# A fused attention and MLP block on one core: x tiles with their own homes, loads placed between transpositions, and W2 loads tied to W1 items

## The chip, the core and the metric

The kernel runs on one core of a Trainium2 chip. Five engines work on their own instruction queues: TensorE (PE, matrix products; its weight loads are listed as PEld), VectorE (DVE), ScalarE (ACT), GpSimd (POOL) and SyncE (SP), which issues all the kernel's DMAs. The metric is the device time of one execution in microseconds; the profile counts its span from the first to the last instruction of the program.

## The reference

Input x is 2048 rows of 1024. The reference normalizes the rows, runs an attention block and an MLP on the normalized rows, and joins both:

```python
x = A_x
xn = _layernorm(x, axis=-1)
s = _A_ref(xn, A_wqkv, A_wo)                       # 32 heads of 32, softmax(q k^T / sqrt(32)) v, then @ wo
g = _silu(_B_ref(xn, B_w1, B_b1, B_w2, B_b2))      # gelu(layernorm(xn) @ w1 + b1) @ w2 + b2, hidden width 3584
return x + s * g
```

Everything is bf16 in memory; the products accumulate in f32.

## The kernel before

**Tiling.** The 2048 rows are 16 tiles of 128 (`t`), or 8 pairs of 256 (`n`, `qb`, `kp`). The 32 heads are 8 groups of four (`hg`). `xnT` holds the normalized x transposed, 8 blocks of 128 columns (`dc`). The score work is cut into *units* (`unit`): for one head group, one block of 256 queries and one of 256 keys, eight matmuls (line 846) fill four of six PSUM banks, and two ScalarE activations of 1024 columns (line 855) write the exponentials into a `P` buffer. There are 8 x 8 x 8 = 512 units, so about a thousand such activations. Values and row sums are matmuls of `P` (line 612); in head group 0 the first three query blocks sum with eight extra matmuls for each unit (`plain`), later ones mostly by adds on VectorE (`tree`).

**The prologue.** For each tile: load x (`load_x`) into a home `xst`, mean and variance, `rs` = (variance + eps)^-0.5 by a GpSimd power (line 794), normalize on VectorE into one of four `xnb` (`normalize`). Statistics come from two `bn_stats` and a `bn_aggr` on VectorE; for tile `AT` = 1 ScalarE makes them, with a Copy and a Square that also sum (line 769), and VectorE finishes them with three small instructions. Tiles 0 to 3 (`NTR` = 4) are transposed by TensorE (`tr_item`) and copied to `xnT` by ScalarE (line 737); tiles 4 to 15 are transposed by DMA from SyncE (line 752). The homes of x are ten blocks of `hT`, so tiles 10 to 15 take the home of a tile ten before; their loads wait for the normalization of an earlier tile (`first[...]`).

`q_item` and `k_item` make Q and K of head group 0 for one pair in 16 matmuls of 256 columns; the K goes to SBUF by ScalarE (line 722), the Q by VectorE (line 712). `v_item` makes V for head groups 0 and 1 with `wv`. The units of group 0 follow in a written order (`order0`), (0,0), (0,1), (1,0), (1,1), (0,2) and so on, as query block and key block; a key block must be there before its first unit.

**The MLP.** `make_y` loads x rows again into `yst`, normalizes them and transposes them by DMA into `yT`; `w1_item` multiplies by W1 from a ring of three 512 KB buffers and writes `hT`; `w2_item` multiplies by W2 from a ring of four 448 KB buffers. These items are woven into the attention. Buffers are shared over time: the W1 and W2 rings, a part of `hT` and others first hold exponentials of head group 0, which `after(...)` orders.

**What sets the order.** `_Plan` records every operation with its engine, a cost, a priority and its dependencies, then runs a greedy list scheduler (`run`) over them: ScalarE prefers exponentials, TensorE prefers score units that are ready and fills with dense items by position and due time. SyncE's DMAs are ordered by the same planner, with a modelled bandwidth. What comes out is a fixed order of instructions on each engine; `settle` and `emit` add the semaphore waits. So an edit in the prologue can reorder everything behind it. While TensorE would be idle early on, the planner puts filler matmuls (line 668). A part of the program draws on a fixed number to break ties (`seeds`); it is the same in both kernels.

## Time and profile before

| | |
|---|---|
| median of three runs | 1037.83 us (1036.45 to 1039.3) |
| the profiled execution | 1036.92 us, span 1035.1 us |
| TensorE busy | 1006.4 us, 97% |
| ScalarE busy | 1016.2 us, 98% |
| VectorE busy | 941.4 us, 91% |
| GpSimd busy | 11.5 us, 1% |
| first exponential starts | 12.70 us |
| DMA, whole span | 168.01 MB, 162 GB/s on the mean |
| granted TensorE clock | 0.998 |

A timeline line gives the start and the length in us, the engine (PE, PEld, DVE, ACT, POOL; SPq is SyncE issuing DMAs), the source line, the operation, the tile written and those read, the shapes, how many like it follow one another, and in brackets the idle time before the first of them with what ended it. A line of the page's groups gives in the end busy time, mean length, and idle time before. A landing is the time from the issue of a DMA to its completion. A wait on several semaphores is put down to the one that came last.

### The profile page before, as it was taken

What the parts mean: (1) busy time and instruction counts of PE and PEld (TensorE: products, weight loads), DVE (VectorE), ACT (ScalarE), POOL (GpSimd) and SP (SyncE); (2) the same over time, 40 slices, a digit from 0 to 9 for tenths busy, and PEclk for the clock granted to TensorE, in tenths of its full rate; (3) what the DMA queues carried; (4) which work ended last, traced back from release to release, by engine and by line L of the source; (5) the groups of instructions that cost most, each with busy time, mean ns of one, the idle gap of its engine ahead of it and who ended that gap; (6) DMA issues with size and microseconds to landing.
All of it is one profiled execution on the core that took longest, in us unless ns stands there. A gap on an engine that the chain in (4) does not pass through costs nothing.

```text
span 1035.1 us, 31895 instructions
## 1 busy us (share of the span) xinstructions
PE 1006.4 (97%) x14329; PEld 637.8 (62%) x14329; DVE 941.4 (91%) x1321; ACT 1016.2 (98%) x1093; POOL 11.5 (1%) x21
## 2 busy tenths in 40 slices
...
GB/s 204 173 225 109 183 169 165 182 111 154 184 185 166 179 151 220 134 151 193 136 130 175 146 222 168 161 178 153 122 148 160 216 169 87 269 232 121 107 94 60
DMA packets 318200, 168.01 MB, mean 162 GB/s; under 512 B 56688, under 2 KB 306032, under 8 KB 318064
## 3 DMA queue, kind: packets, MB, share of 16 engines
...
q8 instruction: 112, 1.84, 0.8%
...
## 4 chain that ended last, share of the span: by engine, by line
ACT 88%; PE 8%; DVE 2%; DMA 1%; issue 1%; SPq 0%; POOL 0%; DVEq 0%
ACT P L855 81%; PE ps L617 4%; ACT ut L1039 4%; PE ps L612 2%; ACT gw L1066 1%; PE ps L846 1%; ACT P L1156 1%; DVE stats L785 1%; DMA xnT<-gw 0%; DMA hT<-in_A_x_dram 0%; DVE gw L748 0%; DVE PA L872 0%; DVE hT L1369 0%; DVE gw L1067 0%; DVE ut L1036 0%
## 5 line engine op out<-in xcount | busy, mean ns | idle before, releaser
L855 ACT ACTIVATE P<-ps 128x1024 bf16<-128x1024 f32 x988 | 923.0, 1223 | 4.7 <-PE ps L846 4.6
L872 DVE TENSOR_TENSOR PA<-P 128x2048 bf16<-128x2048 bf16 x173 | 210.1, 1217 | 32.0 <-ACT P L855 31.5
L617 PE MATMUL ps<-yT,w1r 128*128 128x256 bf16 x1792 | 228.4, 274 | 0.3
L617 PE MATMUL ps<-w2r,hT 128*128 128x256 bf16 x1792 | 223.6, 274 | 1.4 <-DMA w2r<-in_B_w_dram 1.1
L886 DVE TENSOR_TENSOR PR<-PR,PA 128x2048 bf16<-128x2048 bf16 x173 | 209.4, 1212 | 1.2
L846 PE MATMUL ps<-QKT 32*128 32x256 bf16 x4032 | 200.3, 273 | 9.8 <-ACT P L855 7.8
L617 PEld LDWEIGHTS ps<-yT,w1r 128*128 128x128 bf16 x1792 | 164.4, 98 | 53.3 <-issue 29.7
L617 PEld LDWEIGHTS ps<-w2r,hT 128*128 128x128 bf16 x1792 | 163.1, 98 | 51.4 <-issue 31.2
L846 PEld LDWEIGHTS ps<-QKT 32*128 32x128 bf16 x4032 | 59.9, 92 | 139.2 <-ACT P L855 129.2
L612 PE MATMUL ps<-P,V 128*32 128x256 bf16 (+1 forms) x4080 | 138.0, 272 | 0.0
L617 PE MATMUL ps<-xnT,wqk 128*128 128x512 bf16 (+1 forms) x560 | 131.0, 362 | 3.2 <-DMA xnT<-gw 1.3
L612 PEld LDWEIGHTS ps<-P,V 128*32 128x32 bf16 x4080 | 95.9, 96 | 31.6 <-issue 22.0
L617 PE MATMUL ps<-wv,xnT 128*128 128x256 bf16 (+1 forms) x576 | 87.6, 286 | 0.6 <-DVE hT L1022 0.3
L617 PEld LDWEIGHTS ps<-xnT,wqk 128*128 128x128 bf16 x560 | 49.5, 98 | 53.3 <-issue 14.3
L1022 DVE TENSOR_TENSOR hT<-ps,b1T 128x512 bf16<-128x512 f32 x112 | 76.7, 685 | 2.3 <-PE ps L617 1.5
L872 DVE TENSOR_TENSOR PR<-P 128x2048 bf16<-128x2048 bf16 x60 | 72.9, 1215 | 0.3 <-ACT P L855 0.2
L617 PEld LDWEIGHTS ps<-wv,xnT 128*128 128x128 bf16 x576 | 52.5, 98 | 24.8 <-issue 11.4
L1039 ACT ACTIVATE ut<-ut 128x2048 bf16<-128x2048 bf16 (+1 forms) x33 | 61.8, 1871 | 0.0
L941 DVE STREAM_TRANSPOSE nt<-ps 128x256 f32<-128x256 f32 x63 | 28.0, 444 | 13.8 <-PE ps L612 13.6
L702 DVE CAST QKT<-ps 128x512 bf16<-128x512 f32 x58 | 39.8, 685 | 0.6 <-PE ps L617 0.2
L1041 DVE TENSOR_TENSOR hT<-ut,hT 128x2048 bf16<-128x2048 bf16 (+1 forms) x33 | 34.7, 1052 | 0.2
L1036 DVE TENSOR_TENSOR ut<-hT 128x2048 bf16<-128x2048 bf16 (+1 forms) x33 | 34.8, 1053 | 0.1
...
## 6 DMA issues: line engine op xcount, KB each, us to landing
w1r<-in_B_w_dram SPq DMA_DIRECT2D x112, 512.0 KB, 4.5
w2r<-in_B_w_dram SPq DMA_DIRECT2D x128, 448.0 KB, 4.6
...
```

Of the source, the lines that this page charges most:

```text
L612: ins = e.matmul(dst(j), lhsT=lhsT(j), rhs=rhs(j), start=start, stop=stop, tile_position=(0, 32 * j), skip_group_check=True)
L617: return e.matmul(dst, lhsT=lhsT, rhs=rhs, start=start, stop=stop, skip_group_check=True)
L702: dve(lambda e: e.tensor_copy(QKT[sl][:, which, tq * 512:(tq + 1) * 512], bank(it.bank)), c_ps(512), [], [(nm, sl, 2 * tq), (nm, sl, 2 * t ...
L846: ins = e.matmul(bank(b0[j], kk * 256, (kk + 1) * 256), lhsT=QKT[sl][32 * j:32 * j + 32, 1, kb * 128:(kb + 1) * 128], rhs=QKT[sl][32 * j:3 ...
L855: x = act(lambda e, h=h: e.activation(Pt[pi][:, 2 * h:2 * h + 2].rearrange("p j k q -> p (j k q)"), ps[:, pr[h] * 1024:(pr[h] + 1) * 1024] ...
L872: return dve(lambda e: e.tensor_tensor(dst[:].rearrange("p u j q -> p (u j) q"), src[:].rearrange("p u j k q -> p (u j) k q")[:, :, 0, :], ...
L886: return dve(lambda e: e.tensor_tensor(fl3(pr), fl3(pr), fl3(PA[i]), op=ALU.add), c_b16(2048), [("PA", i), tok], [tok], 3.2)
L941: dve(lambda e: e.transpose(nt_t[:], bank(pv.bank, 256, 512)), c_ps(256) + 120, [], [("nt",)], prio, pv)
L1022: dve(lambda e: e.tensor_tensor(hT[:, hs], bank(it.bank).rearrange("p (k t) -> p k t", k=2), b1T[:, 2 * pi:2 * pi + 2].unsqueeze(2).to_bro ...
L1036: dve(lambda e: e.tensor_tensor(u_, x_, x_, op=ALU.mult), c_b16(n), hs_, [("ut", ui)], gp)
L1039: act(lambda e: e.activation(u_, u_, ACT.Tanh, scale=GC), c_acts(n), [("ut", ui)], [("ut", ui)], ga)
L1041: dve(lambda e: e.tensor_tensor(x_, u_, x_, op=ALU.mult), c_b16(n), [("ut", ui)] + hs_, hs_, gp)
```

## The change

Seven edits:

1. Each x tile has its own home: ten in `hT` as before, four in the two `PR` buffers, two in the `yst` buffers. The first real users of `PR` and `yst` wait for the reads of these tiles.
2. Tiles 4 to 11 are loaded at once (before: 4 to 9). Tiles 12 and 13 are loaded once tile 7 is normalized, 14 and 15 once tile 9 is; the order on SyncE comes out as: tiles 4 to 11, transposes 4 and 5, `wv`, transposes 6 and 7, tile 12, transposes 8 and 9, tiles 13 and 14, transposes 10 and 11, tile 15, transposes 12 to 15. Before it was: tiles 4 to 9, `wv`, transposes 4 and 5, tiles 10 and 11, transposes 6 to 9, tiles 12 to 15, transposes 10 and 11, one `wqk`, the first two `yst`, transposes 12 to 15.
3. The first load of `wv` waits for the normalization of tile 5; the K weights of head group 1 wait for that of tile 15 (before: 9).
4. `AT` = (1, 3): the statistics of tile 3 are made on ScalarE as well.
5. The first pair's Q and K are made tile by tile in one item (`qk_first`), with 128-column matmuls, the K in bank 1; `k_item(1)` also works tile by tile. The planner may put a TensorE transposition into an open dense item.
6. The `yst` loads of chunk 0 no longer wait for tile 11; those of chunk 1 wait for W1 item 4.
7. The four W2 loads of the first W2 item wait for W1 items 4, 6, 8 and 10. On SyncE they come behind w1 loads; before, all four stood behind the third w1 load.

```diff
@@ -317,6 +317,13 @@
                 use = "v"
             elif d_ok:
                 use = "d"
+            tq, th = self.dense["tr"], heads["tr"]
+            if use is None and S["do"] is not None and th < len(tq) and tq[th].chunks[0].left == 0 and tq[th].chunks[0].ready <= t:
+                heads["tr"] += 1
+                tq[th].k = 1
+                S["mode"] = "d"
+                commit(tq[th].chunks[0], t)
+                return
             if use is None:
                 nxt = min(nxt, v_at, d_at)
                 bf = bank_for() if S["do"] is None and S["pvo"] is None and nxt > t + 250 and t > self.fill0 else None
@@ -498,7 +505,7 @@
         o_d = nc.dram_tensor("o_scratch", (HG, 128, S), BF16).ap()
 
         NP, NPX, NPA, NH, NW1R, NW2R = 10, 16, 3, 20, 3, 4
-        NTR, NWARM, NG0, AT = 4, 8, 3, 1
+        NTR, NWARM, NG0, AT = 4, 8, 3, (1, 3)
         ident = sb("ident", [128, 128], BF16)
         ones = sb("ones", [128, 32], BF16)
         xnT = sb("xnT", [128, DC, S], BF16)
@@ -544,6 +551,10 @@
             Pt.append(h_flat[:, (3 + i) * 2048:(4 + i) * 2048].rearrange("p (j k q) -> p j k q", j=4, k=2))
         NXS = 10
         xst = [h_flat[:, i * 1024:(i + 1) * 1024] for i in range(NXS)]
+        for i in range(2):
+            pr_flat = PR[i][:].rearrange("p u j q -> p (u j q)")
+            xst += [pr_flat[:, 0:1024], pr_flat[:, 1024:2048]]
+        xst += [yst_t[i][:] for i in range(2)]
         xnb = [gw[:, i * 1024:(i + 1) * 1024] for i in range(4)]
         iota_i = ut_t[0][:].rearrange("p a b -> p (a b)")[:, 0:256].bitcast(I32)
 
@@ -617,13 +628,13 @@
             return e.matmul(dst, lhsT=lhsT, rhs=rhs, start=start, stop=stop, skip_group_check=True)
 
 
-        XS = lambda t: ("xst", t % NXS)
+        XS = lambda t: ("xst", t)
 
         def fl3(t):
             return t[:].rearrange("p u j q -> p (u j q)")
 
         def load_x(t, extra=()):
-            dma(f"x{t}", lambda e: e.dma_start(xst[t % NXS], x2[t * 128:(t + 1) * 128, :]), 262144, [], [XS(t)],
+            dma(f"x{t}", lambda e: e.dma_start(xst[t], x2[t * 128:(t + 1) * 128, :]), 262144, [], [XS(t)],
                 rate=390.0, prio=2, occ=500, lat=2450, extra=extra)
 
         nqk = {"n": 0}
@@ -635,17 +646,16 @@
             dma(f"wqk{i}", lambda e: e.dma_start(wqk[i][:], src), 262144, [], [("wqk", i)], prio=2, rate=228.0, extra=extra)
             return i
 
-        def load_v(pr):
+        def load_v(pr, extra=()):
             src = A_wqkv[:, 2 * D + pr * 256: 2 * D + (pr + 1) * 256].rearrange("(c p) n -> p c n", p=128)
-            dma("wv", lambda e: e.dma_start(wv[:], src), 524288, [], [("wv",)], prio=2, rate=200.0)
+            dma("wv", lambda e: e.dma_start(wv[:], src), 524288, [], [("wv",)], prio=2, rate=200.0, extra=extra)
 
         for t in range(NTR):
             load_x(t)
         wk0 = load_qk(0, 1)
         wq0 = load_qk(0, 0)
-        for t in range(4, NXS):
+        for t in range(NTR, 12):
             load_x(t)
-        load_v(0)
         pool(lambda e: e.iota(iota_i, pattern=[[1, 128]], base=0, channel_multiplier=-1), 300, [], [("ut", 0)])
         dve(lambda e: e.tensor_single_scalar(ident[:], iota_i, 0, op=ALU.is_equal), 220, [("ut", 0)], [("ident",)], 0)
         dve(lambda e: e.memset(ones[:], 1.0), 90, [], [("ones",)], 0)
@@ -715,12 +725,27 @@
 
         def k_item(n):
             it = _Item("pro", 0.01 * n)
-            for dc in range(DC):
-                def fn(e, b, dc=dc):
-                    return mm(e, bank(b, 0, 256), wqk[wk0][:, dc, :], xnT[:, dc, n * 256:(n + 1) * 256], dc == 0, dc == DC - 1)
-                chunk(it, fn, Q256, [("xnT", 2 * n, dc), ("xnT", 2 * n + 1, dc), ("wqk", wk0)])
+            for lo, w in ((0, 128), (128, 128)) if n < 2 else ((0, 256),):
+                for dc in range(DC):
+                    def fn(e, b, dc=dc, lo=lo, w=w):
+                        at = n * 256 + lo
+                        return mm(e, bank(b, lo, lo + w), wqk[wk0][:, dc, :], xnT[:, dc, at:at + w], dc == 0 and lo == 0, dc == DC - 1)
+                    chunk(it, fn, Q256 if w == 256 else Q128, [("xnT", 2 * n + i, dc) for i in range(lo // 128, (lo + w) // 128)] + [("wqk", wk0)])
             act(lambda e: e.activation(QKT[0][:, 1, n * 256:(n + 1) * 256], bank(it.bank, 0, 256), ACT.Copy), c_act(256), [],
                 [("K", 0, n)], -1, it)
+            return it
+
+        def qk_first():
+            it = _Item("pro", -0.001)
+            for lo, d0, d1 in ((0, 0, 8), (128, 0, 4), (128, 4, 8)):
+                for k, wi in ((0, wq0), (1, wk0)):
+                    for dc in range(d0, d1):
+                        def fn(e, b, dc=dc, lo=lo, k=k, wi=wi):
+                            return mm(e, bank(k or b, lo, lo + 128), wqk[wi][:, dc, :], xnT[:, dc, lo:lo + 128],
+                                      dc == 0 and lo == 0, dc == DC - 1)
+                        chunk(it, fn, Q128, [("xnT", lo // 128, dc), ("wqk", wi)], [("S", 0, 1)] if k else ())
+            dve(lambda e: e.tensor_copy(QKT[0][:, 0, 0:256], bank(it.bank, 0, 256)), c_ps(256), [], [("Q", 0, 0)], 0, it)
+            act(lambda e: e.activation(QKT[0][:, 1, 0:256], bank(1, 0, 256), ACT.Copy), c_act(256), [("S", 0, 1)], [("K", 0, 0)], -1)
             return it
 
         def tr_item(t):
...
-            first[t] = dve(lambda e: e.tensor_scalar(xnb[t % 4], xst[t % NXS], mv[:, t, 0:1], lnp[:, t, 1:2],
+            first[t] = dve(lambda e: e.tensor_scalar(xnb[t % 4], xst[t], mv[:, t, 0:1], lnp[:, t, 1:2],
...
@@ -762,33 +787,35 @@
                 plan.readers.setdefault(x, []).extend(got)
 
         for n in range(NPR):
+            if n >= 6:
+                for t in (2 * n, 2 * n + 1):
+                    load_x(t, [first[7] if n == 6 else first[9]])
             groups = [(2 * n,), (2 * n + 1,)] if n < 2 else [(2 * n, 2 * n + 1)]
             for ts in groups:
-                if ts == (AT,):
+                if ts[0] in AT:
+                    a_ = ts[0]
                     for k, f, sc in ((0, ACT.Copy, 1.0 / D), (1, ACT.Square, D ** -0.5)):
-                        act(lambda e, k=k, f=f, sc=sc: e.activation(
-                            fl3(PA[0])[:, k * 1024:(k + 1) * 1024], xst[AT], f, scale=sc, accum_out=mv[:, AT, k:k + 1]),
-                            c_acts(1024) + 93, [XS(AT)], [("st", AT, k)], 1)
-                    dve(lambda e: e.tensor_tensor(lnp[:, AT:AT + 1, 2], mv[:, AT:AT + 1, 0], mv[:, AT:AT + 1, 0], op=ALU.mult), 65,
-                        [("st", AT, 0)], [("s2",)], 0.95)
-                    dve(lambda e: e.scalar_tensor_tensor(lnp[:, AT:AT + 1, 0], mv[:, AT:AT + 1, 1], EPS, lnp[:, AT:AT + 1, 2], op0=ALU.add,
-                                                         op1=ALU.subtract), 65,
-                        [("st", AT, 1), ("s2",)], [("ve", AT)], 0.95)
-                    dve(lambda e: e.tensor_tensor(mv[:, AT:AT + 1, 1], mv[:, AT:AT + 1, 1], lnp[:, AT:AT + 1, 2], op=ALU.subtract), 65,
-                        [("st", AT, 1), ("s2",)], [("mv", AT)], 1.1)
+                        act(lambda e, k=k, f=f, sc=sc, a_=a_: e.activation(
+                            fl3(PA[a_ // 2])[:, k * 1024:(k + 1) * 1024], xst[a_], f, scale=sc, accum_out=mv[:, a_, k:k + 1]),
+                            c_acts(1024) + 93, [XS(a_)], [("st", a_, k)], 1)
+                    dve(lambda e, a_=a_: e.tensor_tensor(lnp[:, a_:a_ + 1, 2], mv[:, a_:a_ + 1, 0], mv[:, a_:a_ + 1, 0], op=ALU.mult), 65,
+                        [("st", a_, 0)], [("s2", a_)], 0.95)
+                    dve(lambda e, a_=a_: e.scalar_tensor_tensor(lnp[:, a_:a_ + 1, 0], mv[:, a_:a_ + 1, 1], EPS, lnp[:, a_:a_ + 1, 2],
+                                                                op0=ALU.add, op1=ALU.subtract), 65,
+                        [("st", a_, 1), ("s2", a_)], [("ve", a_)], 0.95)
+                    dve(lambda e, a_=a_: e.tensor_tensor(mv[:, a_:a_ + 1, 1], mv[:, a_:a_ + 1, 1], lnp[:, a_:a_ + 1, 2], op=ALU.subtract),
+                        65, [("st", a_, 1), ("s2", a_)], [("mv", a_)], 1.1)
                 for t in ts:
-                    if t == AT:
+                    if t in AT:
                         continue
-                    if t >= NXS:
-                        load_x(t, [first[2 * n - 5]])
                     for c in range(2):
-                        dve(lambda e, t=t, c=c: e.bn_stats(stats[:, t, c, :], xst[t % NXS][:, c * 512:(c + 1) * 512]),
+                        dve(lambda e, t=t, c=c: e.bn_stats(stats[:, t, c, :], xst[t][:, c * 512:(c + 1) * 512]),
...
-                if ts != (AT,):
+                if ts[0] not in AT:
...
@@ -797,9 +824,12 @@
                     normalize(t, rs)
             if n < NTR // 2:
                 plan.dense["tr"] += [tr_item(2 * n), tr_item(2 * n + 1)]
-            if n < NG0:
-                pro_q.append(q_item(n))
-            pro_q.append(k_item(n))
+            if n == 0:
+                pro_q.append(qk_first())
+            else:
+                if n < NG0:
+                    pro_q.append(q_item(n))
+                pro_q.append(k_item(n))
...
+        load_v(0, [first[5]])
...
-             rss + [("mv", t) for t in range(NT)], [("s2",)], 2)
+             rss + [("mv", t) for t in range(NT)], [("s2",), ("s2", AT[0]), ("s2", AT[1])], 2)
...
@@ -963,7 +994,7 @@
 
 
         def proj(hg, w):
-            wk = load_qk(hg, 1, [first[9]] if hg == 1 else ())
+            wk = load_qk(hg, 1, [first[NT - 1]] if hg == 1 else ())
...
@@ -984,17 +1015,18 @@
...
+        w1_ev = {}
...
-        def load_w2(q, r):
+        def load_w2(q, r, extra=()):
...
-            dma(f"w2{i}", lambda e: e.dma_start(w2r[:, i], src), 458752, [], [("w2", i)], lat=3100.0)
+            dma(f"w2{i}", lambda e: e.dma_start(w2r[:, i], src), 458752, [], [("w2", i)], lat=3100.0, extra=extra)
...
@@ -1002,7 +1034,7 @@
             for t2 in range(2):
...
                 dma(f"yx{t2}", lambda e, t=t, t2=t2: e.dma_start(yst_t[t2][:], x2[t * 128:(t + 1) * 128, :]), 262144, [],
-                    [("yst", t2)], rate=390.0, extra=[first[11]] if c == 0 else ())
+                    [("yst", t2)], rate=390.0, extra=[w1_ev[4]] if c == 1 else ())
...
@@ -1019,7 +1051,7 @@
...
-            dve(lambda e: e.tensor_tensor(hT[:, hs], bank(it.bank).rearrange("p (k t) -> p k t", k=2),
+            w1_ev[p] = dve(lambda e: e.tensor_tensor(hT[:, hs], bank(it.bank).rearrange("p (k t) -> p k t", k=2),
...
@@ -1112,12 +1144,15 @@
                     it = w1_item(s_[1], s_[2])
                 else:
                     for r in range(4):
-                        w2slot[(s_[1], s_[2], r)] = load_w2(s_[2], r)
+                        w2slot[(s_[1], s_[2], r)] = load_w2(s_[2], r, [w1_ev[(4, 6, 8, 10)[r]]] if s_[1] + s_[2] == 0 else ())
                     it = w2_item(s_[1], s_[2])
                 it.pos = pos
                 (mq if s_[0] == "w1" else plan.dense["w2"]).append(it)
 
 
+        for i in range(2):
+            after([("PR", i)], [XS(10 + 2 * i), XS(11 + 2 * i)])
+            after([("yst", i)], [XS(14 + i)])
         pvs = [_Item("pv") for _ in range(NG0)]
         order0 = [(0, 0), (0, 1), (1, 0), (1, 1), (0, 2), (1, 2), (2, 0), (2, 1)]
         for kp in range(3, NKP):
```

## The prediction

> **What bounds the kernel now.** I read the page first, then ScalarE (ACT) in order of time, then who made it wait. The page:
>
> ```profile
> span 1035.1 us, 31895 instructions
> ...
> PE 1006.4 (97%) x14329; PEld 637.8 (62%) x14329; DVE 941.4 (91%) x1321; ACT 1016.2 (98%) x1093; POOL 11.5 (1%) x21
> ...
> q8 instruction: 112, 1.84, 0.8%
> ...
> ACT 88%; PE 8%; DVE 2%; DMA 1%; issue 1%; SPq 0%; POOL 0%; DVEq 0%
> ...
> L855 ACT ACTIVATE P<-ps 128x1024 bf16<-128x1024 f32 x988 | 923.0, 1223 | 4.7 <-PE ps L846 4.6
> ```
>
> ScalarE is busy 98%, nearly all of it exponentials, and the chain runs through it. What the change can win is therefore ScalarE's idle time, 18.9 us. The timeline of ScalarE alone (start, length, idle before) shows where it lies:
>
> ```profile
> 4.22 1.06 ACT L769 ACTIVATE PA<-hT 128x1024 bf16<-128x1024 bf16 x1 [2.00 <-DMA hT<-in_A_x_dram]
> ...
> 7.39 1.02 ACT L737 ACTIVATE xnT<-ps 128x1024 bf16<-128x1024 bf16 x1 [0.98 <-PE ps L733]
> 9.01 2.07 ACT L737 ACTIVATE xnT<-ps 128x512 bf16<-128x512 bf16 x3 [0.60 <-PE ps L733]
> 11.81 0.38 ACT L722 ACTIVATE QKT<-ps 128x256 bf16<-128x256 f32 x1 [0.72 <-PE ps L617]
> 12.70 1.02 ACT L855 ACTIVATE P<-ps 128x1024 bf16<-128x1024 f32 x1 [0.51 <-PE ps L846]
> ...
> 16.66 4.69 ACT L855 ACTIVATE P<-ps 128x1024 bf16<-128x1024 f32 x5 [0.51 <-PE ps L846]
> 22.55 0.38 ACT L722 ACTIVATE QKT<-ps 128x256 bf16<-128x256 f32 x1 [1.19 <-PE ps L617]
> ...
> 37.96 1.02 ACT L855 ACTIVATE P<-ps 128x1024 bf16<-128x1024 f32 x1 [0.73 <-PE ps L846]
> ...
> 64.32 3.77 ACT L855 ACTIVATE P<-ps 128x1024 bf16<-128x1024 f32 x4 [1.11 <-PE ps L846]
> 69.80 31.39 ACT L855 ACTIVATE P<-ps 128x1024 bf16<-128x1024 f32 x34 [1.71 <-PE ps L846]
> ```
>
> From 69.8 us to the last 8 us no gap is listed: in hundred-microsecond windows ScalarE is busy 99.98 to 100.00 of 100. The last 45 rows of the built order are the same for TensorE, VectorE and SyncE, and so are ScalarE's last 19; so a microsecond won before 70 us should arrive at the end. Removable are the gaps from 7.39 to 69.80, 8.3 us with the 0.22 at 15.77.
>
> The last two gaps come from TensorE, which stops inside a block of eight matmuls and waits for nothing:
>
> ```profile
> 61.29 0.28 PE L612 MATMUL ps<-V,ones 128*32 128x256 bf16 x2
> ...
> 63.10 0.40 PE L612 MATMUL ps<-V,ones 128*32 128x256 bf16 x6 [1.53 <-issue]
> ...
> 69.03 0.40 PE L612 MATMUL ps<-P,ones 128*32 128x256 bf16 x6 [1.70 <-issue]
> ```
>
> Between these stops lie 128 matmuls and 128 weight loads, 256 instructions. The page's 112 packets of 16 KB on q8 are one for each 256 of TensorE's 28,658. So these are waits for instructions: the packets that end them begin at 60.42 and 66.50 in the trace, 4.1 and 3.4 us after TensorE crossed the boundary before, and TensorE goes on 1.5 us after each packet's end. From 67 us on no such stop recurs; later boundaries lie some 10 us apart and most packets begin within 0.5 us. At 60 to 64 us the DMA moved 333 GB/s, and SyncE had just queued this:
>
> ```profile
> 57.87 2.13 SPq L1004 DMA_DIRECT2D yst<-in_A_x_dram  x2
> 60.04 0.43 SPq L991 DMA_DIRECT2D w1r<-in_B_w_dram  x1
> 60.51 7.85 SPq L997 DMA_DIRECT2D w2r<-in_B_w_dram  x4
> ```
>
> **The change part by part.** The sum is against the profiled execution: 1036.92 us, span 1035.1, 0.91 below the median 1037.83 of the three runs.
>
> *Tile 3's statistics go to ScalarE, the first pair goes tile by tile.* Removed from VectorE: two bn_stats (0.6 each), an aggregate (0.11) and the +eps (0.06), 1.4 us; added, three small ones at 0.07. Added on ScalarE: what tile 1 costs there, 4.22 to 6.40, 2.18 us. I lay it out by the built order: sums for 3 at 6.32 (x3 landed at 6.19), xnT of tile 0 at 7.45 (was 7.39), squares for 3 at 8.37, xnT of tile 1 at 9.42 (9.01), xnT of 2 at 10.5 (10.0), K copy 11.55 (11.81), xnT of 3 at 12.25 (13.62), first exponential 13.2 (12.70), second K copy 14.1 (15.77), second exponential 14.4 (14.52), third 15.3 (16.66). So the new work fills idle time, delays the first exponential 0.5 and brings the third 1.35 us earlier. The 48 matmuls of 128 columns for 24 of 256 (0.06 each by the fillers' spacing, against 0.11) cost TensorE nothing. The Q copy moves behind a bn_stats on VectorE, to 12.05; it lies under the xnT of tile 3.
>
> *Transposes of tiles 4 and 5.* They are issued when normalized, about 0.7 us earlier (14.9 against 15.65), since VectorE is freer. The second took 4.4 us to land with two x loads beside it and 2.8 when four ran alone; now wv's load is issued behind it. It lands at 19.2 to 20.7 (was 21.41). Eight exponentials are done at 20.8, so the third K copy starts between 20.8 and 21.85; I take 21.1. After it I count the 0.5 us before a score unit again. Ninth exponential: 22.0 against 23.75, gain 1.75 (bounds 1.0 and 1.95).
>
> *Loads in steps.* The 0.73 gap at 37.96 follows the transposes of tiles 10 and 11, issued right behind four x loads:
>
> ```profile
> DMA to landing us min/median/max: 6.1/6.4/6.6
> ```
>
> Four others, at 21 to 27 us, took 2.8. They landed 2.4 and 3.3 us after the last x load. In the new order two x loads (13, 14) stand directly before them and the issue is at about 27.4: landing near 33.5 instead of 37.11, when ScalarE, 2 us ahead, needs the K at about 33. I take 0.3 of the 0.73 (bounds 0 and 0.7). Tiles 12 to 15 follow as now, without a gap before and hence none counted.
>
> *wv behind those transposes.* It lands at 17.7 plus 4.7 to 6.2 us, 22.4 to 23.9; the V matmuls ahead of the seventh unit want it by 24.1. Cost nothing; the cover is thin, and each microsecond past it is one on ScalarE, up to 1. The wqk and first y loads also move back, but the y rows land with about 1 us to spare and are normalized only for W1 items that began at 71.86. The homes in PR and yst change only addresses.
>
> *W2 and second y loads after W1 items.* They leave 2.3 MB out of the rush at 58 to 68 us. In the built order both boundaries still lie after the 24th and the 26th unit, now some 2.2 us earlier, and only three w1 loads and wv precede them; the first two w1 loads are issued near 51.5. The packet wanted at 58.9 should come at 57.7 to 59.7, the one wanted at 64.5 long before. Of 2.82 us I take 2.3 (bounds 0, if the packets come as late as now, and 2.82). In their new place each W2 load is 448 KB, 1.5 us at 300 GB/s, in front of w1 loads that landed 1.4 to 4.3 us before use at 100 to 122 us: nothing, or 0.5 where it just misses.
>
> Sum: 1.75 + 0.3 + 2.3 = 4.35 gained. 1036.92 - 4.35 = 1032.6 on the profile's scale, 1033.5 on the median's; I say 1033.2.
>
> *Where the notes speak against it.* TensorE stood 1.53 and 1.70 us at a boundary of 256 instructions. The Trainium skill (Runtime: NRT & Kernel Launch, "Instruction fetch mechanics") says that crossing such a boundary is "mostly hidden", and gives TensorE a buffer of eight blocks. By this nothing would be won from the W2 move, and the sum would be that of the first rival. In the trace a packet begins after its boundary and is for the next one, so I follow the rows. The skill's page DMA: Bandwidth & Descriptors ("Queues, rings and completion order") adds that each engine takes turns between queues; then a fetch would hardly wait behind SyncE's backlog, and the backlog would not be the cause. The 4.1 and 3.4 us against under 0.5 with a light load speak for the backlog, without proving W2's part; the rival below has its price.
>
> **The rivals.**
> - *The fetch waits stay.* Something other than W2 makes the packets late, or wv and w1 do it as well: the packet at 60.42 began when only wv, wqk, y transposes and w1 had been queued at its request. Only the prologue's 2.05 is won: 1034.9, on the median's scale 1035.8. For it: the first stop; against it: the second stop, with only W2, y and one w1 load outstanding.
> - *The prologue gives nothing.* ScalarE's 2.18 us come before the first exponential, and the transposes of 5 and 11 land as late as now. Then 2.3 is won: 1034.6 (1035.5). Against it: the walk above wins 1.35 before any DMA transpose matters.
> - *Slower: W1 starves.* W2 loads took 6.8 us to land at the median before 100 us, one 8.4. If each of the four holds a w1 load behind it for 8.4 - 4.2 us, less about 2 us of slack, TensorE, which runs in order, stops about 2.2 us four times, and the scores queued behind stop ScalarE: 8.8 - 4.35 = 4.4 us slower, 1041.3. It decides from a hold of about 1.1 us over the slack, four times. Against it: DMA share is 0.54 at 60 to 100 us, and no wait for w1 is listed anywhere.
>
> **How the numbers follow.** Forecast 0.68, fetch waits stay 0.12, no prologue gain 0.08, slower 0.12. The range reaches down to all removable idle time less the statistics, 8.3 - 2.2 = 6.1 (1030.8; I write 1030.5), and up to past the two half gains, 1037. The bound of 0.3% is 3.1 us. Nine tenths of the forecast's chance and a quarter of the half gains lie beyond it: faster 0.66. The half gains' rest and the forecast's tail are within: 0.23. Slower 0.11.
>
> **What would show it.** Right: ScalarE's third exponential near 15.3 and ninth near 22; no "issue" idle over 0.6 us on TensorE at 50 to 70 us; no listed gap on ScalarE after 66. Wrong: statistics of tile 3 holding up xnT of tile 1 by more than 0.5; a gap of over 1 us before the third K copy; TensorE waiting for w1 or wv; new gaps past 70 us, where the whole middle is ordered anew.

## The result and the profile after

The changed kernel takes 1039.46 us (median, 1037.2 to 1040.7); the kernel before, on the same chip, took 1036.45. The ratio is 1.002, 95% interval [1.0012, 1.0029]: slower by 0.2%, where I forecast 1033.2 us and a range up to 1037. By the measure of 2% that is no change. But 4.35 us were expected to be won, so some 6 us are to be explained.

The profiled execution took 1040.15 us (before: 1036.92). From its page:

```profile
span 1038.3 us, 31853 instructions
...
PE 998.3 (96%) x14271; PEld 636.7 (61%) x14341; DVE 938.3 (90%) x1320; ACT 1018.1 (98%) x1097; POOL 11.6 (1%) x21
...
ACT 83%; PE 10%; DVE 3%; DMA 2%; issue 1%; POOL 0%; DVEq 0%; another core or an unknown queue 0%; POOLq 0%
...
L886 ACT ACTIVATE P<-ps 128x1024 bf16<-128x1024 f32 x988 | 922.9, 1221 | 4.3 <-PE ps L877 4.2
```

ScalarE is still the bound and its exponentials cost the same (922.9 us). It is busy 1.9 us more, mostly with the statistics of tile 3. TensorE ran 14,341 matmuls (by its weight loads; some matmul records are missing) against 14,329: twelve more, a number that will matter. ScalarE in order of time (start, length, idle before):

```profile
13.14 1.02 ACT L886 ACTIVATE P<-ps 128x1024 bf16<-128x1024 f32 x1
14.04 0.39 ACT L734 ACTIVATE QKT<-ps 128x256 bf16<-128x256 f32 x1
14.31 6.55 ACT L886 ACTIVATE P<-ps 128x1024 bf16<-128x1024 f32 x7
22.30 0.38 ACT L734 ACTIVATE QKT<-ps 128x256 bf16<-128x256 f32 x1 [1.45 <-PE ps L628]
23.41 3.77 ACT L886 ACTIVATE P<-ps 128x1024 bf16<-128x1024 f32 x4 [0.73 <-PE ps L877]
...
36.05 1.02 ACT L886 ACTIVATE hT<-ps 128x1024 bf16<-128x1024 f32 x1 [0.97 <-PE ps L877]
...
48.70 1.02 ACT L886 ACTIVATE w1r<-ps 128x1024 bf16<-128x1024 f32 x1 [0.81 <-PE ps L877]
...
59.90 9.30 ACT L886 ACTIVATE P<-ps 128x1024 bf16<-128x1024 f32 x10 [1.55 <-PE ps L877]
70.09 6.67 ACT L886 ACTIVATE P<-ps 128x1024 bf16<-128x1024 f32 x7 [0.90 <-PE ps L877]
...
1032.97 0.60 ACT L1396 ACTIVATE PR<-ps 128x512 bf16<-128x512 f32 x1 [4.58 <-PE ps L628]
```

The walk to the eighth exponential came out to 0.1 us. Then the third K copy waits 1.45 us, two gaps follow that the kernel before had smaller or not at all, and the two gaps near 60 and 70 us are still there. The last wait has become 4.58; in the kernel before it was

```profile
1029.53 0.60 ACT L1361 ACTIVATE PR<-ps 128x512 bf16<-128x512 f32 x1 [2.76 <-PE ps L617]
```

TensorE in the changed kernel at those places:

```profile
21.22 1.81 PE L628 MATMUL ps<-xnT,wqk 128*128 128x256 bf16 x15 [1.74 <-DMA xnT<-gw]
...
35.40 0.27 PE L628 MATMUL ps<-xnT,wqk 128*128 128x256 bf16 x1 [1.17 <-DMA xnT<-gw]
...
58.79 0.29 PE L623 MATMUL ps<-P,ones 128*32 128x256 bf16 x3 [1.39 <-issue]
...
68.99 0.29 PE L623 MATMUL ps<-P,ones 128*32 128x256 bf16 x3 [1.05 <-issue]
...
1028.80 0.39 PE L623 MATMUL ps<-P,ones 128*32 128x128 bf16 x15
1030.39 0.22 PE L623 MATMUL ps<-P,ones 128*32 128x128 bf16 x1 [1.20 <-issue]
```

These are waits on DMA transpositions (tiles 5 and 11), the two instruction stops, and a third stop ahead of the last matmul of the last group, on the path to the end. Some words for what follows: a *packet* is a transfer of 16 KB, 256 instructions, on TensorE's instruction queue q8; a *boundary* is a place in TensorE's program where one such block of 256 ends; an *instruction stop* is idle time of TensorE at a boundary, listed as "issue".

ScalarE's idle time by stretch (width of the window less ScalarE's busy time in it, in us; the wait near the end apart). The last two columns are experiments told below:

| stretch, us | before | after | after, 48 fillers fewer | before, 36 fillers fewer |
|---|---|---|---|---|
| 0 to 13 | 5.54 | 3.29 | 3.51 | 5.84 |
| 13 to 26 | 1.92 | 2.17 | 1.36 | 1.06 |
| 26 to 46 | 0.73 | 1.05 | 0.57 | 0.18 |
| 46 to 56 | 0 | 0.81 | 0 | 0 |
| 56 to 75 | 2.92 | 2.45 | 0.52 | 0 |
| 75 to 112 | 0 | 1.02 | 0.13 | 0 |
| 112 to 1020 | 0.04 | 0.08 | 0.58 | 0.18 |
| the wait near the end | 2.76 | 4.58 | 2.75 | 2.76 |
| ScalarE busy, in all | 1016.2 | 1018.1 | 1017.5 | 1015.5 |

Before 13 us the change fills 2.25 us of idle time, nearly all with the new work (ScalarE's 1.9 us more). After that it wins only 0.47 (56 to 75) and loses 0.25 + 0.32 + 0.81 + 1.02 + 1.82.

### The profile page after: what moved, and what is told of

It reads as the page before. It is cut to its first block, busy times and chain, and to the rows that moved or that the text cites. A ratio compares the mean times of both kernels' runs of the same rounds, so it can differ in the third digit from the quotient of the medians.

```text
span 1038.3 us, 31853 instructions
## 1 busy us (share of the span) xinstructions
PE 998.3 (96%) x14271; PEld 636.7 (61%) x14341; DVE 938.3 (90%) x1320; ACT 1018.1 (98%) x1097; POOL 11.6 (1%) x21
## 4 chain that ended last, share of the span: by engine, by line
ACT 83%; PE 10%; DVE 3%; DMA 2%; issue 1%; POOL 0%; DVEq 0%; another core or an unknown queue 0%; POOLq 0%
ACT P L886 76%; PE ps L628 6%; ACT ut L1071 4%; PE ps L623 2%; PE ps L877 2%; ACT gw L1098 1%; ACT P L1191 1%; DMA xnT<-gw 1%; DMA yst<-in_A_x_dram 1%; DMA w2r<-in_B_w_dram 1%; PE ps L678 0%; DVE PA L903 0%; DVE hT L1054 0%; DVE PR L917 0%; DVE stats L812 0%
## 5 line engine op out<-in xcount | busy, mean ns | idle before, releaser
L886 ACT ACTIVATE P<-ps 128x1024 bf16<-128x1024 f32 x988 | 922.9, 1221 | 4.3 <-PE ps L877 4.2
L628 PE MATMUL ps<-xnT,wqk 128*128 128x512 bf16 (+2 forms) x530 | 119.1, 351 | 8.0 <-DMA xnT<-gw 2.9
```

Of the source, the lines that this page charges most:

```text
L628: return e.matmul(dst, lhsT=lhsT, rhs=rhs, start=start, stop=stop, skip_group_check=True)
L886: x = act(lambda e, h=h: e.activation(Pt[pi][:, 2 * h:2 * h + 2].rearrange("p j k q -> p (j k q)"), ps[:, pr[h] * 1024:(pr[h] + 1) * 1024] ...
```

## The experiments

All kernels that follow leave only such matmuls out as write nothing that is used (warm-up matmuls and the fillers that keep TensorE running while it would wait); none leaves out work of the reference. Ratios are to the kernel before on the same chip, which took 1036.1 to 1037.2 us there; kernels of different chips are compared by ratio. A time inside a profile is one execution's: the kernel before and the first kernel of experiment 2 run the same instructions up to 57 us, and their exponentials stand 0.2 to 0.4 us apart there; so smaller differences between two profiles are not read. Several kernels also differ in more than the part that is asked about, since an edit that adds, drops or reorders matmuls shifts what the later boundaries fall on.

### 1. The last block of instructions

My theory on the end: the twelve extra matmuls push a boundary between two 256-instruction blocks into the last group. I took seven warm-up matmuls out of the changed kernel, and put twelve into the kernel before.

```
         def warm_fn(e, b):
-            for _ in range(NWARM):
+            for _ in range(1):
...
-            for _ in range(NWARM):
+            for _ in range(20):
```

The first edit is in the changed kernel, the second in the kernel before. `NWARM` itself stays 8, so the planner writes the same order.

> The changed kernel, with 7 of its 8 warm-up matmuls at the start left out (they write nothing that is used); the planned order is otherwise the same on every engine. Theory 'boundary at the end': the changed kernel has 14341 matmuls against 14329, so TensorE's last boundary of 256 instructions falls into the last block of row-sum matmuls, where it stood 1.20 us; with 7 fewer the program ends before it. Then that stop is gone, the last idle time of ScalarE falls from 4.58 to about 2.8 us and the time by 1.5 us, to about 1038.0. Rival 'late work on VectorE or in the out stores': the end stays at 4.58 us and the time does not change (within 0.3 us). In the early part the boundaries lie 7 matmuls further on in the code; both expect stops of 1 to 1.5 us near 58 and 69 us as before.

> The kernel before, with 20 warm-up matmuls instead of 8, so 14341 in all; nothing else changes. Theory 'boundary at the end': a stop of about 1.2 us appears in the last block of row sums, ScalarE's last idle time rises from 2.76 to about 4.5 us, and the time rises by 1.5 us. Rival 'other late work': no change of the end. The two stops at 61 and 67 us stay in both, within 0.5 us, their place 12 matmuls earlier in the code.

Changed kernel with one warm-up: 1037.76 us, 1.001 [1.0001, 1.002]. The last wait:

```profile
1032.94 0.60 ACT L1396 ACTIVATE PR<-ps 128x512 bf16<-128x512 f32 x1 [2.76 <-PE ps L628]
```

So 1.8 us of the 4.58 were the boundary, in the profile; in the medians half of the loss, some 1.0 us. Nothing else of this profile can be used to size the change: it is the slowest of the kernel's executions (1040.42 us), with a granted TensorE clock of 0.5 for 3.4 us from 37.4 us on. The kernel before with twelve more: 1037.6, 1.0009 [1.0, 1.0018]. Its last wait is 3.19, not 4.6: there the boundary lies ahead of the last two matmuls of the kernel, where TensorE waits for VectorE in any case, and it cost 0.4 us; what makes up the rest of the 0.9 is not known. The mechanism holds; its price depends on what the boundary falls on.

### 2. The later W2 and second y loads, alone and undone

```
-                        w2slot[(s_[1], s_[2], r)] = load_w2(s_[2], r)
+                        w2slot[(s_[1], s_[2], r)] = load_w2(s_[2], r, [w1_ev[(4, 6, 8, 10)[r]]] if s_[1] + s_[2] == 0 else ())
...
-                    [("yst", t2)], rate=390.0, extra=[first[11]] if c == 0 else ())
+                    [("yst", t2)], rate=390.0, extra=[first[11]] if c == 0 else [w1_ev[4]] if c == 1 else ())
```

The first kernel puts this into the kernel before. The second takes it out of the changed kernel (with one warm-up).

> The kernel before with the MLP part of the change alone: the four W2 loads of the first W2 item wait for W1 items 4, 6, 8 and 10, the second y loads for W1 item 4. The prologue is that of before. Theory 'W2 and y loads delay the instruction packets': both stops of TensorE at 61 and 67 us shrink below 0.5 us, ScalarE loses its gaps of 1.11 and 1.71 us, and stands 2.3 to 2.8 us earlier at 80 us. Rival 'wv, y transposes and w1 loads delay them': the first stop stays at 1 us or more, the second shrinks to 0 to 1; ScalarE stands 0.5 to 1.7 us earlier at 80 us. The new order after 80 us may give some of it back: the changed kernel lost 1.35 us there at its 91st exponential.

> The changed kernel without its MLP part (W2 and second y loads as early as the planner wants), and 7 warm-up matmuls fewer so that the end has no boundary. Theory 'the MLP part wins': stops at 58 to 70 us grow from 2.4 to 3 us or more against the changed kernel. Rival 'it is neutral': the stops stay at 2 to 2.5 us. Theory 'order of W1 and W2 work costs 1.35 us at the 91st exponential': without the MLP part that loss is gone. The time against the kernel before: 0 to +1.5 us.

Alone: 1036.12, 0.9994 [0.9984, 1.0005]. The instruction stops fell from 3.2 us to 0.8, and ScalarE's idle time at 56 to 75 us from 2.92 to 0.55: the 2.3 us of the prediction, in the profile. The median shows 0.7 us won, with an interval that takes in no change at all.

```profile
56.95 0.40 PE L612 MATMUL ps<-P,ones 128*32 128x256 bf16 x6 [0.37 <-issue]
62.59 0.40 PE L612 MATMUL ps<-V,ones 128*32 128x256 bf16 x6 [0.44 <-issue]
```

Undone in the changed kernel: 1038.54, 1.0018 [1.0006, 1.003], against 1.001 with it; the stops at 50 to 72 us are 3.7 us in sum against 2.0. Both pairs point to a gain and neither median is clear of the noise; nothing here says that this part makes the change slow. ScalarE's idle time at 75 to 112 us, 1.02 in the changed kernel, is nothing without this part.

### 3. Loads, homes, compute: one part at a time

Five kernels ask which other part loses. (a) All x loads and wv issued at once, ahead of the first transposition, instead of in steps (here and in (b) with one warm-up matmul, to be compared with the 1.001 of experiment 1):

```
-        for t in range(NTR, 12):
+        for t in range(NTR, 10):
+            load_x(t)
+        load_v(0)
+        for t in range(10, 16):
             load_x(t)
...
-        load_v(0, [first[5]])
```

> The changed kernel with one part undone in another way: the loads of all x tiles and of wv are issued at once, ahead of the first DMA transposition (order x4 to x9, wv, x10 to x15), instead of in steps between the transpositions; and one warm-up matmul instead of eight, so that no fetch boundary lies in the last block of matmuls (the warm-up matmuls write nothing that is used). Theory A, loads beside a transposition delay its landing: the transpositions of tiles 5, 10 and 11, which took 4.9, 5.6 and 5.2 us from issue to landing, take about 2.8 to 3.3 us; the ScalarE gaps at 22.3 and 23.4 us (1.45 and 0.73) shrink by 1 us or more in sum and the one at 36.05 (0.97) goes; exponentials 10 to 43 come 1 to 2 us earlier than in the changed kernel, and the time is 1 to 2 us below that of the changed kernel with one warm-up matmul (1037.76), so 1036 to 1036.8. Theory B, a transposition has to wait for all transfers that were issued before it: the first pair (tiles 4 and 5) now lands later than 21.2 us, the gap ahead of the third K copy grows by 1 us or more and the time is 1038 to 1040. Theory C, the transpositions are slow by themselves: they take 5 us as before, and nothing moves by more than 0.5 us.

1038.85, 1.0028 [1.0017, 1.0038], the highest ratio of all. Theory B held for the first pair and A for the later ones:

```profile
26.33 0.38 ACT L737 ACTIVATE QKT<-ps 128x256 bf16<-128x256 f32 x1 [5.66 <-PE ps L628]
27.98 3.77 ACT L885 ACTIVATE P<-ps 128x1024 bf16<-128x1024 f32 x4 [1.26 <-PE ps L876]
```

Tile 4's transposition, issued at 14.70, landed at 22.70: the last x load before it was under way until 20.43, an instruction packet followed until 21.66. Tiles 8 and 9, with nothing about, took 2.7 and 2.8. But tiles 10 and 11 took 4.5 and 4.1 us with no load anywhere near; only a packet (35.94 to 37.49) lay between the issue of tile 10's transposition and its landing. That row did not fit my theory, and led to experiment 5.

(b) The changed kernel with tiles 14 and 15 in the third probability buffer instead of the two yst buffers. The first y loads then need not wait for tile 15:

```
-        xst += [yst_t[i][:] for i in range(2)]
+        xst += [PA[2][:].rearrange("p u j q -> p (u j q)")[:, i * 1024:(i + 1) * 1024] for i in range(2)]
...
-                    [("yst", t2)], rate=390.0, extra=[w1_ev[4]] if c == 1 else ())
+                    [("yst", t2)], rate=390.0, extra=[first[11]] if c == 0 else [w1_ev[4]] if c == 1 else ())
```

> The changed kernel with other homes for tiles 14 and 15 (the third probability buffer PA[2] instead of the two yst buffers), and the first two y loads again wait only for the normalised tile 11, as before the change; one warm-up matmul instead of eight. Theory A, the y chain moved into the time of the fetch packets keeps the two instruction stops at 58.8 and 69.0 us (1.39 and 1.05 us): the y loads land near 39 instead of 50 to 51 us, the first two w1 loads are issued before 56 us, and the issue stops of TensorE between 50 and 70 us fall to 1.2 us or less in sum; exponentials 55 to 86 come about 1.2 to 2 us earlier than in the changed kernel, and the time is 1036 to 1036.8 against the 1037.76 of the changed kernel with one warm-up matmul. Rival B, the stops follow where the 16 KB blocks end and wv alone, not y: the stops stay above 2 us in sum and the time stays within 0.5 us of 1037.76.

1035.24, 0.9992 [0.9984, 1.0001], against 1.001: 1.8 us won, more than hoped. TensorE's instructions are the same in the same order as in the changed kernel with one warm-up, so the boundaries fall on the same work. SyncE in the changed kernel, and then with the other homes (start, time to issue):

```profile
46.45 1.05 SPq L1036 DMA_DIRECT2D yst<-in_A_x_dram  x2
...
48.03 3.40 SPq L855 DMA_DIRECT2D b2b<-in_B_b_dram  x1
...
51.95 3.47 SPq L1041 DMA_TRANSPOSE yT<-yst  x1
55.47 0.58 SPq L651 DMA_DIRECT2D wv<-in_A_wqkv_dram  x1
...
58.70 1.71 SPq L1023 DMA_DIRECT2D w1r<-in_B_w_dram  x2
```

```profile
32.47 1.76 SPq L1036 DMA_DIRECT2D yst<-in_A_x_dram  x2
...
49.63 2.97 SPq L1041 DMA_TRANSPOSE yT<-yst  x1
52.65 0.58 SPq L651 DMA_DIRECT2D wv<-in_A_wqkv_dram  x1
...
55.83 1.64 SPq L1023 DMA_DIRECT2D w1r<-in_B_w_dram  x2
```

The y loads go out 14 us earlier, and what queues behind them 2 to 3 us. ScalarE's idle time at 56 to 75 us is 0.40 us.

(c) The kernel before with the compute part alone (statistics of tiles 1 and 3, the first pair tile by tile), and (d) the same with the later W2 loads; both with four warm-ups, homes and loads of x as before.

```
-        NTR, NWARM, NG0, AT = 4, 8, 3, 1
+        NTR, NWARM, NG0, AT = 4, 8, 3, (1, 3)
...
-            pro_q.append(k_item(n))
+            if n == 0:
+                pro_q.append(qk_first())
+            else:
+                if n < NG0:
+                    pro_q.append(q_item(n))
+                pro_q.append(k_item(n))
```

> The kernel before with the compute part of the change alone: ScalarE statistics of tiles 1 and 3, Q and K of the first pair tile by tile, K of the second pair in two halves, and transpositions of the first tiles taken as soon as they are ready. Homes and loads of the x tiles, the y, w1 and W2 loads stay as before. Four warm-up matmuls instead of eight, so that no fetch boundary lies in the last block of matmuls. Theory A, the compute part wins what was predicted of it and the loads in steps lose it again: the ninth exponential starts 1.5 us earlier than before (22.2 against 23.75), exponentials 16 to 49 about 1.0 to 1.7 us earlier too, the instruction stops at 61 and 67 us stay (2.5 to 3 us in sum), and the time is 1034.8 to 1035.8 against the 1036.45 to 1036.8 of before. Rival B, the win is lost at the next late transposition whatever the loads do: by exponential 34 less than 0.5 us is left, and the time is within 0.5 us of before.

> The kernel before with the compute part and the part that makes the W2 and the second y loads later; homes and loads of the x tiles as before, four warm-up matmuls instead of eight. It leaves out of the change only the x tiles' own homes and the loads in steps. Theory A, the two parts win independently: 1.5 us of the compute part and the 0.3 to 2.2 us that the later W2 loads alone gave, so 1033 to 1035, with less than 1 us of instruction stops on TensorE between 50 and 70 us. Rival B, the second win goes when the first comes (the stops reappear, because the fetch packets are wanted earlier and still come at the same time): 1035 to 1036.5, with stops of 2 us or more in sum.

(c): 1035.07, 0.9996 [0.9986, 1.0006]; (d): 1035.41, 0.9995 [0.9986, 1.0004]. In (c) the fourth exponential comes 1.56 us earlier than before, the tenth still 0.90, the 43rd 0.76. At the 49th it is 2.08, but the added 1.3 us are not the compute part's: TensorE's stops are 1.2 us in sum, not the 3.2 of the kernel before that I expected to stay, with the W2 loads in their old place. So in the profile the compute part wins about half of what A has, and the ratio's interval takes in nothing won. In (d) the stops go (0.4 us), but no second win shows.

(e) The late y loads by themselves, put into (d):

```
-                    [("yst", t2)], rate=390.0, extra=[first[11]] if c == 0 else [w1_ev[4]] if c == 1 else ())
+                    [("yst", t2)], rate=390.0, extra=[first[15]] if c == 0 else [w1_ev[4]] if c == 1 else ())
```

> The kernel before with the compute part and the later W2 loads (which took 1035.4 us), and with the first two y loads made to wait for the normalised tile 15 instead of tile 11; homes and loads of the x tiles as before. This does the late y loads by themselves, without the loads in steps. Theory A, the late y loads cost the changed kernel 1.8 us, since b2's broadcast, yT, wv and the first w1 loads queue behind them on SyncE and the 16 KB instruction packets then come late: the y loads land at 48 us or later instead of 39 to 40, the first w1 load is issued 2 to 3 us later than 56.3, TensorE's issue stops between 50 and 70 us rise from 0.4 to 2 us or more, and the time is 1036.8 to 1037.5. Rival B, lateness of y alone is hidden and the cost needs the x loads in steps with it: the stops stay under 1 us and the time is within 0.5 us of 1035.4.

1039.62, 1.0017 [1.0005, 1.0029], against 0.9995 without it: 2.2 us, theory A, and more than the 1.4 to 2.1 us that it named. Its ScalarE and TensorE:

```profile
60.13 1.94 ACT L881 ACTIVATE P<-ps 128x1024 bf16<-128x1024 f32 x2 [2.50 <-PE ps L872]
```

```profile
58.81 0.29 PE L619 MATMUL ps<-P,V 128*32 128x256 bf16 x3 [2.26 <-issue]
```

The packet for this stop was wanted at 52.22 and began at 56.38, with the y loads, b2, wv, wqk and the first yT on the queue; in the kernel before the packet at this place waited 1.8 us. A second cost followed in this profile: after the stop the granted clock was 0.5 from 60.2 to 63.6 us, and eight K matmuls took 1.76 us (1.05 at full clock in experiment 2's first kernel). How much of the 2.2 us in the medians is the stop and how much the clock is not known.

### 4. Two edits that should have mended the transpositions

In kernel (b), wv issued right after x9 instead of behind tile 5's transposition; then the planner told that transpositions of tiles 10 to 15 land 1.8 us later; then both.

```
-        load_v(0, [first[5]])
...
-                    [("xnb", t % 4)], [("xnT", t, c) for c in range(DC)], prio=0, rate=300.0, occ=1300, lat=1000)
+                    [("xnb", t % 4)], [("xnT", t, c) for c in range(DC)], prio=0, rate=300.0, occ=1300, lat=2800 if t >= 10 else 1000)
```

> The changed kernel with tiles 14 and 15 in the third probability buffer and one warm-up matmul (1035.24 us), and with the first wv load issued right after x9, ahead of x10, x11 and every DMA transposition, instead of behind the transposition of tile 5. Nothing else is moved by hand. Theory A, the transposition of tile 5 lands late (4.7 us after issue) because wv's 512 KB are issued beside it: it now lands 2.8 to 3.3 us after issue if the loads ahead of it are through by then, at 19.6 to 20.3 us instead of 21.36, the ScalarE gaps at 22.5 and 23.6 us (1.22 and 0.72) shrink by 1 us or more, and the time is 1034 to 1034.6. Rival B, transpositions wait for every load issued before them: the transposition of tile 4 lands at 19.5 us or later instead of 18.2, tile 5 one us behind it, and the gap stays or grows; time 1035 to 1036. Rival C, tile 5 is late by itself (being second): still about 4.5 us from issue to landing with nothing beside it.

> The changed kernel with tiles 14 and 15 in the third probability buffer and one warm-up matmul (1035.24 us), where the planner is told that the transpositions of tiles 10 to 15 take 1.8 us longer than it took them to (lat 2800 instead of 1000), as the trace shows of tiles 10, 11 and 15. No transfer is added or moved by hand; only the written order of the matmuls may follow. Theory A, the gaps at 36 and 48 us are score units queued in TensorE's written order behind K matmuls whose tiles have not landed: the K matmuls of tiles 10 to 15 stand later in the order, the ScalarE gaps at 35.98 and 48.43 (0.73 and 0.61) go, exponentials 25 to 49 come 0.7 to 1.3 us earlier, and the time is 1034 to 1034.6. Rival B, the K matmuls placed later delay their own K copies and with them the score units of those tiles: new gaps of the same size 2 to 6 us later, time 1035 to 1036.

> Both of the two edits before in one kernel: tiles 14 and 15 in the third probability buffer, one warm-up matmul, wv issued right after x9, and the planner told 1.8 us more for the transpositions of tiles 10 to 15. Theory A, the two win independently and this is the fastest of the family: 1033 to 1034, with less than 2 us of ScalarE idle between 13 and 56 us (3.4 in the kernel with the other homes alone). Rival B, what the one wins is only later idle time for the other: 1034.5 to 1035.5.

wv first: 1036.48, 0.9993 [0.9984, 1.0002], as without it. Tile 5 took 4.63 us though wv had landed before its issue (16.25 against 16.54) and the last load beside it, x11, was through at 17.55: theory A, that wv delays it, fell, and C was left. The planner's value: 1037.16, 1.0003 [0.9991, 1.0014], no gain; the gap at 36 us went, but two early gaps grew (in kernel (b) they are 1.22 and 0.72):

```profile
23.09 0.38 ACT L734 ACTIVATE QKT<-ps 128x256 bf16<-128x256 f32 x1 [2.09 <-PE ps L628]
25.15 3.77 ACT L886 ACTIVATE P<-ps 128x1024 bf16<-128x1024 f32 x4 [1.67 <-PE ps L877]
```

The edit did not put them there: every engine has the same instructions in the same order as in (b) up to 35 us. TensorE ahead of the first of these gaps, here and then in (b):

```profile
21.59 2.96 PE L628 MATMUL ps<-xnT,wqk 128*128 128x256 bf16 x15 [1.97 <-DMA xnT<-gw]
```

```profile
21.40 1.81 PE L628 MATMUL ps<-xnT,wqk 128*128 128x256 bf16 x15 [1.51 <-DMA xnT<-gw]
```

The granted clock was 0.5 from 22.1 to 25.5 us in this execution and 1.00 in (b), behind a wait for tile 5 that was half a us longer. So this profile says little about the planner's value. Both edits: 1035.28, 0.9984 [0.9974, 0.9995], by the ratio 0.8 us below (b) with overlapping intervals; ScalarE's idle time between 13 and 56 us is 2.7 us, not under 2, so rival B fits better than A.

### 5. Moving the block boundaries and nothing else

The rows that no load explains had one thing in common: a 16 KB instruction packet for TensorE between the issue and the landing of the transposition. So the next kernels leave out the filler matmuls that the planner writes between 15 and 21.5 us of its own time. Every other instruction of every engine keeps its place in the order, but each later boundary falls 46 to 48 matmuls later in the work (36 in the kernel before).

```
-                if bf is not None and bf[0] <= t and t > 20000.0 and active(t) >= self.fill:
+                if bf is not None and bf[0] <= t and (t > 20000.0 and active(t) >= self.fill or 15000.0 < t < 21500.0):
```

First kernel (b) again, as a control on the same chip, then (b) with fillers left out:

> The same kernel as the one with tiles 14 and 15 in the third probability buffer, again, as the reference on the same chip for the next two. Both theories expect of it what it showed: 1 us below before, the transposition of tile 5 landing 4.7 us after issue, tile 15 4.9 us.

> That kernel with 48 filler matmuls fewer on TensorE between 15 and 25 us (they write nothing that is used and stand where TensorE would wait), and nothing else changed: no DMA, no other instruction moves. So the boundaries between the 256-instruction blocks come 48 matmuls later in the work: the second one, passed at 18.4 us, is passed near 23 us, after the transposition of tile 5, and the fourth one, passed at 44.05, near 49 us, after that of tile 15. Theory A, a 16 KB instruction packet that comes while a transposition is under way or queued holds its landing up (a transposition with such a packet has landed 1.0 to 2.0 us after the packet's end, one without it 2.7 to 3.6 us after its issue): tile 5 lands 2.8 to 3.4 us after issue, at 19.4 to 20.1 us instead of 21.36, tile 15 at 45.0 to 45.6 instead of 47.58, the ScalarE gap of 1.22 us ahead of the third K copy falls below 0.3 and the one at 48.4 goes; exponential 10 starts 1.0 to 1.9 us earlier than in the control on the same chip, and the time is 0.5 to 1.5 us below it. Theory B, it is wv's load beside it that delays tile 5: nothing changes, 4.7 us from issue to landing, time within 0.5 us. Theory C, without the fillers TensorE's clock falls and the matmuls of 20 to 30 us take longer: the mean of a 128x256 matmul there rises above 0.13 us, and the time is above the control's.

The landings did what A said. The view of the DMA from the issue of tile 5's transposition to its landing, in the control:

```profile
DMA  9999999400089999999900999000000001999999
...
q8 instruction: 1, 0.02, 1.9%
...
xnT<-gw SPq DMA_TRANSPOSE x2, 3.9
```

and without the fillers:

```profile
DMA  9999999999994000005999999999999610000311
...
q1 hardware_dynamic: 2079, 0.52, 81.7%
...
xnT<-gw SPq DMA_TRANSPOSE x1, 2.8
```

The first line is the busy share of the DMA engines in tenths, in forty slices; q8 is TensorE's instruction queue. With the packet (18.30 to 19.72) tile 5 took 4.77 us, and for eight slices in a row, 19.4 to 20.4, the engines are all but idle (0 to 11 GB/s): it is not bandwidth that is short. In the last 0.65 us of them, after the packet's end, 22 transfers of 256 bytes follow one another. That would fit one DMA engine that carried the packet and has its share of the transposition still to do; the trace does not tell the engines apart. Without the packet, 2.83, with wv's load issued just the same. Tile 15 went from 4.94 to 2.80. ScalarE's wait ahead of the third K copy is 0.21 (1.33 in the control), the tenth exponential 0.86 us earlier, the gaps at 36 and 48 us gone. Not all of C is wrong: the granted clock was 0.5 from 18.4 to 21.9 us, the 21 K matmuls of 20 to 30 us took 340 ns at the mean instead of 274, and the gap behind the K copy grew from 0.72 to 1.19. The time did not follow: 1035.68, 0.9992 [0.9982, 1.0003], control 1035.25, 0.9993. The win of 3.6 us against the kernel before that stood at the 55th exponential (control: 2.3) went later, where TensorE waits for W2:

```profile
685.08 5.61 ACT L886 ACTIVATE P<-ps 128x1024 bf16<-128x1024 f32 x6 [1.18 <-PE ps L877]
```

```profile
683.54 1.16 PE L628 MATMUL ps<-w2r,hT 128*128 128x256 bf16 x9 [1.33 <-DMA w2r<-in_B_w_dram]
```

A second such gap, 0.98 us, stands at 918 us.

The same in the kernel with both edits of experiment 4:

> The fastest kernel so far (wv issued right after x9, the planner told 1.8 us more for the transpositions of tiles 10 to 15, tiles 14 and 15 in the third probability buffer, one warm-up matmul), with the same fillers left out. Theory A (packets hold up transpositions): tile 5 lands at 18.9 to 19.6 us instead of 20.6, exponential 10 starts 1.0 to 1.5 us earlier, and the time is 0.5 to 1.5 us below that kernel's 0.9984 of before, so 0.997 to 0.998. Theory B or C: 0.998 to 1.0 of before, as with the fillers.

1035.54, 0.9996 [0.9987, 1.0005]: the landing as in A (2.83 us), the time as in B or C.

Then in the kernel before, and in the changed kernel as it is:

> The kernel before the change with 36 filler matmuls fewer on TensorE between 16 and 21 us, and nothing else. Its second block boundary, passed at 18.79 us, comes after the landing of tile 5 then, near 22.5 us; its fourth, passed at 44.29 with tiles 14 and 15 under way, near 49 us. Theory A: tile 5 lands at 19.8 to 20.6 us instead of 21.41, tiles 14 and 15 at 44.8 to 46.3 instead of 46.45 and 47.3, exponential 10 starts 0.8 to 1.5 us earlier than before; the total may keep 0 to 1.5 us of it, since the boundaries at 50 to 70 us move too. Theory B: no change of these landings by more than 0.3 us.

> The changed kernel itself, all of it, with 48 filler matmuls fewer between 15 and 25 us on TensorE and nothing else (they write nothing that is used). Theory A: the transpositions of tiles 5 and 15 land 2.8 to 3.5 us after issue instead of 4.9 and 5.1, the last block boundary leaves the last group of matmuls (so the ScalarE wait near the end goes back from 4.58 to about 2.8 us), and the late y loads still cost something between 50 and 70 us: 1036.2 to 1037.5, against 1039.46, so 2 to 3 us of the change's loss go with 48 matmuls that compute nothing. Rival B, the win before 50 us is lost between 50 and 70 us, where packets, y, wv and w1 meet: tail and landings as in A, but 1037.5 to 1039, with issue stops of 3 us or more in sum.

The kernel before without 36 fillers: 1033.26 us, 0.9975 [0.9965, 0.9985]. The changed kernel without 48: 1034.6, 0.9981 [0.9971, 0.999], against 1.002 with them. Matmuls that compute nothing were worth 2.6 us in the one and 4.0 in the other. No kernel left them out and kept the boundaries where they were, so how much of these times is the boundaries and how much the fillers' own place on TensorE is not shown; the landings are. ScalarE in the first:

```profile
21.84 0.43 ACT L722 ACTIVATE QKT<-ps 128x256 bf16<-128x256 f32 x1
22.11 4.75 ACT L855 ACTIVATE P<-ps 128x1024 bf16<-128x1024 f32 x5
...
54.30 22.11 ACT L855 ACTIVATE P<-ps 128x1024 bf16<-128x1024 f32 x24
```

The third K copy does not wait, and from 54.30 on no gap is left until the last wait, with the W2 loads in their old place. Tile 5 took 2.84 us, with two x loads issued beside it as before. In the second:

```profile
21.29 0.38 ACT L734 ACTIVATE QKT<-ps 128x256 bf16<-128x256 f32 x1 [0.21 <-PE ps L628]
...
64.12 12.94 ACT L886 ACTIVATE P<-ps 128x1024 bf16<-128x1024 f32 x14 [0.52 <-PE ps L877]
```

and the last wait is 2.75. Here the y loads are issued at 43.70, 11 us later than with the other homes, and cost little. So the bare lateness of y need not cost; that packets then come late where they are wanted soon is what the stop in 3e shows. I had expected 1036.2 at best.

Last, what the compute part is worth once the packets are out of the way:

> The kernel before with the compute part of the change (as run before: 1035.07 us) and 48 filler matmuls fewer between 15 and 25 us, four warm-up matmuls instead of eight. Asks what the tile-by-tile prologue is still worth once the packets are out of the way. Theory A, it still wins on its own: tile 5 lands at 18.5 to 19.3 us (20.5 in the kernel before without the fillers), exponential 10 starts at least 1 us earlier than there, and the time is 1032 to 1032.8 against that kernel's 1033.26. Rival B, the two have the same gap to close: after the fillers are gone exponential 10 comes 0.2 to 0.6 us earlier at most (the K matmuls of the third pair then wait for ScalarE's own exponentials and a score unit, not for the landing), and the time is within 0.7 us of 1033.26. Rival C, ScalarE, which has 1.9 us more to do with tile 3's statistics, gives the win back: 1034 to 1035.2.

1034.78, 0.998 [0.997, 0.999]. The tenth exponential comes 0.36 us earlier than in the kernel before without fillers, no more than two profiles can differ by; at the 55th it is 1.55 behind (a stop of 1.28 us is left, before 63.19) and stays so. The time is the one that C gave, but the profile puts it down to the stop. The two intervals overlap; nothing shows a gain of the tile-by-tile prologue over the old one here. The kernel before without those fillers has the lowest ratio measured (the next ones overlap with it), and beats both kernels.

## Why the prediction was wrong

*What bounds the kernel; the walk to the eighth exponential.* Right. First exponential 13.14 (13.2 written), second K copy 14.04 (14.1); the third to seventh exponentials come 1.45 to 1.47 us earlier (1.35 written for the third). That it fits to 0.1 us is partly luck: with seven warm-up matmuls fewer the same walk began at 13.68.

*"Transposes of tiles 4 and 5."* The first step that failed. I wrote a landing at 19.2 to 20.7 and the third K copy between 20.8 and 21.85; it landed at 21.17 and the copy began at 22.30, outside the bounds. The ninth exponential gained 0.32, not 1.75. I had put the 4.4 us that tile 5 took in the kernel before down to the two x loads beside it. The rows show a packet from 19.25 to 20.32 in that time, and experiment 5 shows that it is the packet: without it, and with the two x loads, 2.84. The earlier prologue took the boundary along with it, so that the packet met the transposition again, at 17.71 to 19.23.

*"Loads in steps."* 0.3 was taken; the gap grew from 0.73 to 0.97, and one of 0.81 came up at tile 15, for which I had counted none. Tile 11 landed at 35.30 (33.5 written): x14 was under way until 31.92, then came a packet until 33.46. My reading, that a transposition follows the loads issued before it, holds (experiment 3a), but the packet was missing from it, as at tile 15 (44.07 to 46.04; 5.08 us). In the kernel before without fillers tile 10, behind the same four x loads but with no packet, took 4.8 us instead of 6.6.

*"wv behind those transposes", cost nothing.* Right: 23.15, within the bounds, and no wait for it. *"The wqk and first y loads also move back"*, cost nothing: wrong. I looked only at who uses y, and it is used late. Moved past SyncE's queue, it brought yT, wv and w1 with it: the first two w1 loads went out at 58.70, not 51.5. Other homes for two tiles, which let y go early again, won 1.8 us.

*"W2 and second y loads after W1 items."* 2.3 of 2.82 were taken; 0.47 came. The packets that end the two stops began at 56.41 and 66.31, 3.3 and 2.7 us after TensorE had crossed the boundary before, and were needed at 57.4 and 67.9. I had written that the first would come in time or nearly so and the second "long before". In the kernel before the same edit removed 2.37 us of idle time in the profile, so the term was right where y stayed early, and the sum was wrong to add it to a part that refills the same queue. But the mechanism is only half of it: leaving out 36 fillers removed the same stops with the W2 loads untouched. What happened is nearest to the first rival in its second wording, that something else on the queue makes the packets late as well; which transfers do it was not separated.

*"A microsecond won before 70 us should arrive at the end."* Wrong as a rule. I compared the order of the last rows, not the count of instructions ahead of them. Twelve more matmuls cost 1.8 us at the end in the profile and about 1.0 in the medians.

*W1 starves, the slower rival.* Not what happened: no wait for w1 is listed. The change is slower by a mechanism I had for the stops and did not carry to the other places where the same packets come.

*The rest.* The 1.02 at 108 us is TensorE waiting for VectorE's bias additions in the new order; of the two profiles of kernel (b) one has such a gap (0.55) and one has none. The gaps near 685 and 917 us are waits for a W2 load that just misses; a smaller one (0.62, at 689) is there with the W2 loads in their old place too. Neither was tried. Also open: why a packet begins anywhere between 0 and some 5 us after it is wanted, and how the 4.0 us between the changed kernel with and without fillers divide among transpositions, stops and end; the parts do not add, so no division of the 3 us is given.

*What a boundary costs.* The changed kernel has 112 packets and three instruction stops over 1 us, and two transpositions 2 us late behind packets. The Trainium skill (Runtime: NRT & Kernel Launch, "Instruction fetch mechanics") calls the cost of a boundary "mostly hidden". By count these rows agree; the few that are not hidden cost up to 2.3 us each. The same section of the Trainium skill says that the next block is fetched while the current one runs, and the rows agree with that too. The Trainium skill's page DMA: Bandwidth & Descriptors ("Queues, rings and completion order") says that an engine drains a whole packet from one queue before it turns to the next. By this a packet of 1.43 us would cost a transposition up to 1.43 (an estimate); the rows show 1.94 in the pair of kernels that differ in the fillers alone.
